# Second expert product as seven products for eight in parts 2 and 3 of a fused attention and MoE kernel, with the forms of the weights kept in DRAM

## The chip, the cores and the metric

One core of a Trainium2 chip runs the whole kernel in one launch. The time is that of the device from start to end, in microseconds (us); the median of several runs counts. PE is the matrix engine (TensorE), DVE the vector engine, ACT the scalar engine, POOL is GpSimd, SP is the engine that issues all transfers of this kernel. SBUF is the memory beside the engines, PSUM the eight banks of 128x512 fp32 into which PE writes, DRAM the device's main memory.

## The reference

An attention over 4 sequences of 768 tokens with 8 heads of 64, in which a query sees the 4 first keys and the 128 last ones, is followed by a mixture of 8 experts over the N = 3072 tokens of dimension D = 512, with hidden size F = 1024. Every token goes through every expert, weighted by a gate that 8 Sinkhorn iterations balance:

```python
x = attention(q, k, v, n_sink=4, window=128)       # [3072, 512]
P = exp(x @ w_gate - max)
for _ in range(8):
    P /= P.sum(1, keepdims=True) + 1e-09
    P /= P.sum(0, keepdims=True) + 1e-09
    P *= N / E
for e in range(E):
    h = maximum(x @ w1[e], 0.0)
    out += P[:, e:e + 1] * (h @ w2[e])
```

The gate weights are never negative, so weighting `h` by them before the second product gives the same sum as weighting the product.

## The kernel before

Every fp32 operand of a large product is split into a high part (a rounded copy in PE's faster format, made on ACT: a CAST) and a low part (the rest, a subtraction on DVE); `split` does both. A product is then three matmuls, high x high, high x low and low x high.

The tokens go in three parts of 1024 (`NPART`), each in two halves of 512 (`HT`). The weights of an expert go in four units (`NU`) of 256 hidden columns (`UF`). While the attention runs, expert 0 is computed for part 1 in a plain way, in small steps between the attention's (`plain`; its additions are L605). Then come 28 units of part 1 and 32 each of parts 2 and 3, in a pipeline of two stages: in one step PE runs the first product of unit n and the second product of unit n-1. The list `STEPS` interleaves them; a scheduler (the framework's, which orders each engine's instructions by priority and its own estimate of times) places the rest.

- `load_unit` loads a unit's two weight blocks (`r1`, `r2`, 512 KB each), makes sums of blocks on POOL (L715 to L718, tile `ST`), and splits everything into `W1f` (seven forms) and `W2f`.
- The first product is Winograd's form of Strassen's algorithm: a unit's two hidden chunks by two halves of D, times two halves of D by two halves of tokens, in seven products M1 to M7 for eight. Each is 6 matmuls of 128x512 (L771), so 42 in a unit. The forms of x^T that they read (`B11`, `B21`, `B22`, `T1` to `T4`) are made once a part (`load_x`, `make_form`, `fill_form`).
- ACT copies M2, M3 and M5 out of PSUM; DVE adds (L784, tile `C`); ACT and DVE make the split relu (`h`, L779 and L780).
- The second product is plain: eight token tiles by two hidden chunks in sixteen steps of 3 matmuls (L832), 48 in a unit. `weigh` adds each tile to `acc` in SBUF, with the gate weight of its tokens as the factor (L844, DVE). After the last unit of a part `acc` goes out.

Each engine runs its own instructions in order, so an instruction that waits holds those behind it. The order also has every transfer wait for the transfer eight before it.

Of the kernel before, what the change touches and what calls it, by code (L numbers as in the profile page):

```python
# [79 lines left out]
def tile_any_span(ctx: ExitStack, tc: tile.TileContext, q, k, v, span, wg, w1, w2, out):  # L80
    """The whole computation for any n_sink and window."""
# [16 lines left out]
    with ExitStack() as ph:  # L98
# [122 lines left out]
def tile_sink_attention_moe(ctx: ExitStack, tc: tile.TileContext, q, k, v, wg, w1, w2, out):  # L221
    """The computation for n_sink = SINK and window = P."""
# [34 lines left out]
    ident = const.tile([P, P], F32, name="ident")  # L257
    make_identity(nc, ident)
    masks = []
    for t in range(3):  # L260
# [448 lines left out]
    def load_unit(e, u):  # L709
# [216 lines left out]
```

## Time and profile before

| | |
|---|---|
| median of 3 runs | 2238.93 us (2238.04 to 2239.73) |
| span of the profiled execution | 2235.5 us (the page has no other time of it) |
| PE busy | 2213.5 us, 99% |
| DVE, ACT, POOL busy | 1588.4, 899.4, 468.7 us |
| DMA | 140.5 MB in 172567 packets, mean 63 GB/s |

The span runs from the first to the last instruction on the core. The profile's matmul lines give a busy time in which pipelined matmuls overlap; what one costs in a full row is read from the chain of waits, which has them end to end. Windows give, for a stretch, its length and each engine's busy time, with the clock, the DMA engines' busy share and the rate.

### The profile page before, as it was taken

What the parts mean: (1) busy time and instruction counts of PE and PEld (TensorE: products, weight loads), DVE (VectorE), ACT (ScalarE), POOL (GpSimd) and SP (SyncE); (2) the same over time, 40 slices, a digit from 0 to 9 for tenths busy, and PEclk for the clock granted to TensorE, in tenths of its full rate; (3) what the DMA queues carried; (4) which work ended last, traced back from release to release, by engine and by line L of the source; (5) the groups of instructions that cost most, each with busy time, mean ns of one, the idle gap of its engine ahead of it and who ended that gap; (6) DMA issues with size and microseconds to landing.
All of it is one profiled execution on the core that took longest, in us unless ns stands there. A gap on an engine that the chain in (4) does not pass through costs nothing.

```text
span 2235.5 us, 29446 instructions
## 1 busy us (share of the span) xinstructions
PE 2213.5 (99%) x10843; PEld 1838.1 (82%) x10843; DVE 1588.4 (71%) x3010; ACT 899.4 (40%) x1970; POOL 468.7 (21%) x851
## 2 busy tenths in 40 slices
PE   7999999999999999999999999999999999999998
PEld 5888887888888888888888888888888888888887
DVE  8877879766766676867666666667766667666765
ACT  7777763333333333433333333334333333333331
POOL 7655642111111111211111111112111111111100
PEclk9999999999999999999999999999999999999999
DMA  6333422111111111311111111111311111111101
GB/s 172 87 81 90 115 84 87 49 56 57 55 40 57 57 50 45 132 57 48 48 57 57 48 47 57 57 44 42 104 57 39 56 57 57 38 57 57 52 25 39
DMA packets 172567, 140.50 MB, mean 63 GB/s; under 512 B 80256, under 2 KB 141696, under 8 KB 172416
## 3 DMA queue, kind: packets, MB, share of 16 engines
q1 hardware_dynamic: 172416, 138.55, 20.6%
q8 instruction: 87, 1.43, 0.3%
q14 instruction: 64, 0.52, 0.1%
HBM read 125.95 MB, written 12.58 MB: 62 GB/s over the span
## 4 chain that ended last, share of the span: by engine, by line
PE 96%; DVE 2%; ACT 1%; DMA 0%; issue 0%; SPq 0%; POOL 0%; DVEq 0%; POOLq 0%; ACTq 0%
PE o L832 45%; PE c L771 39%; PE O L507 3%; PE ps L450 2%; PE g L581 2%; PE pt L471 1%; PE o L597 1%; PE pt L411 1%; PE O L597 1%; ACT sc L456 0%; PE ps L581 0%; DVE sc L453 0%; DVE PT L338 0%; PE O L537 0%; PE pt L487 0%
## 5 line engine op out<-in xcount | busy, mean ns | idle before, releaser
L832 PE MATMUL o<-W2f,h 128*128 128x512 f32 x4416 | 1073.9, 389 | 0.0
L832 PEld LDWEIGHTS o<-W2f,h 128*128 128x128 f32 x4416 | 828.7, 188 | 172.2 <-DVE acc L844 0.2
L844 DVE SCALAR_TENSOR_TENSOR acc<-o,Pt,acc 128x512 f32<-128x512 f32 x720 | 539.0, 750 | 341.4 <-PE o L832 339.5
L771 PE MATMUL c<-T,W1f 128*128 128x512 f32 x2208 | 561.0, 389 | 0.0
L771 PEld LDWEIGHTS c<-T,W1f 128*128 128x128 f32 x2208 | 414.0, 188 | 86.8 <-DVE C L784 1.0
L779 ACT ACTIVATE h<-C 128x512 fp32r<-128x512 f32 x276 | 174.4, 632 | 638.3 <-DVE C L784 627.3
L771 PE MATMUL c<-B,W1f 128*128 128x512 f32 x1656 | 406.7, 389 | 0.0
L715 POOL TENSOR_TENSOR ST<-r 128x256 f32<-128x256 f32 x92 | 70.0, 761 | 1552.1 <-DMA r<-in_moe_w_dram 1052.8
L771 PEld LDWEIGHTS c<-B,W1f 128*128 128x128 f32 x1656 | 310.5, 188 | 64.8 <-ACT M L797 0.4
L784 DVE TENSOR_TENSOR C<-c,M 128x512 f32<-128x512 f32 x276 | 190.7, 691 | 114.6 <-PE c L771 111.5
L780 DVE SCALAR_TENSOR_TENSOR h<-C,h 128x512 fp32r<-128x512 f32 x276 | 190.0, 688 | 2.7 <-ACT h L779 2.7
L801 ACT COPY M<-c 128x512 f32<-128x512 f32 x92 | 54.0, 587 | 307.0 <-PE c L771 307.0
L779 ACT ACTIVATE h<-c 128x512 fp32r<-128x512 f32 x92 | 55.0, 598 | 247.9 <-PE c L771 247.7
L780 DVE SCALAR_TENSOR_TENSOR h<-c,h 128x512 fp32r<-128x512 f32 x92 | 63.6, 691 | 106.6 <-ACT h L779 106.5
L338 DVE TENSOR_TENSOR W1f<-ST,W1f 128x512 fp32r<-128x512 f32 x184 | 119.6, 689 | 0.0
L338 DVE TENSOR_TENSOR W2f<-r,W2f 128x512 fp32r<-128x512 f32 x184 | 119.1, 686 | 0.0
L456 ACT ACTIVATE sc<-sc,st 128x264 f32<-128x264 f32 x192 | 98.2, 512 | 50.4 <-DVE st L453 49.5
L337 ACT CAST W2f<-r 128x512 fp32r<-128x512 f32 x184 | 113.6, 620 | 6.9 <-PE O L597 6.0
L460 POOL TENSOR_SCALAR sc<-sc,st 128x264 f32<-128x264 f32 x192 | 93.9, 500 | 75.5 <-DVE st L458 58.6
L337 ACT CAST W1f<-ST 128x512 fp32r<-128x512 f32 x184 | 105.2, 620 | 0.0
L338 DVE TENSOR_TENSOR W1f<-r,W1f 128x512 fp32r<-128x512 f32 (+1 forms) x184 | 101.0, 549 | 0.0
L507 PE MATMUL O<-PT,V 128*128 128x256 f32 x528 | 85.1, 294 | 0.9 <-DVE xr L519 0.9
(131 smaller groups left out, 1761.7 us busy)
## 6 DMA issues: line engine op xcount, KB each, us to landing
r<-in_moe_w_dram SPq DMA_DIRECT2D x192, 512.0 KB
xscr<-xr SPq DMA_DIRECT2D x24, 256.0 KB
x<-xscr SPq DMA_DIRECT2D x12, 512.0 KB
out_dram<-acc SPq DMA_DIRECT2D x24, 256.0 KB
kr<-in_k_dram SPq DMA_DIRECT2D x23, 256.0 KB
qr<-in_q_dram SPq DMA_DIRECT2D x23, 256.0 KB
vr<-in_v_dram SPq DMA_DIRECT2D x23, 256.0 KB
vs<-in_v_dram SPq DMA_DIRECT2D x24, 4.0 KB
```

Of the source, the lines that this page charges most:

```text
L337: nc.scalar.copy(dst[:, 0], src)
L338: nc.vector.tensor_sub(dst[:, 1], src, f32(dst[:, 0]))
L456: nc.scalar.activation(sc[:, h, :], sc[:, h, :], AF.Exp, bias=nmx[:, h:h + 1], scale=-1.0, accum_out=sm[:, h:h + 1])
L460: nc.gpsimd.tensor_scalar(sc[:, h, :], sc[:, h, :], rs[:, h:h + 1], 1.0, op0=ALU.mult, op1=ALU.mult)
L507: nc.tensor.matmul(u["O"][:, pr], lhsT=x_, rhs=y_, start=(j == 0), stop=(j == len(ops) - 1))
L715: nc.gpsimd.tensor_add(S[:, 0], A21, A22)
L771: nc.tensor.matmul(ps, lhsT=W1[:, a, i, k, :], rhs=XF[fb][:, b, k, :], start=(start and j == 0), stop=(stop and j == len(ops) - 1), skip_g ...
L779: nc.scalar.activation(h[key][:, 0], src, AF.Relu)
L780: nc.vector.scalar_tensor_tensor(h[key][:, 1], src, 0.0, f32(h[key][:, 0]), op0=ALU.max, op1=ALU.subtract)
L784: nc.vector.tensor_add(C, c1, m)
L832: nc.tensor.matmul(o, lhsT=h[c, th][:, a, off:off + P], rhs=W2[:, w, c, :], start=(c == 0 and j == 0), stop=(c == 1 and j == 2))
L844: nc.vector.scalar_tensor_tensor(acc[i], o_, Pt[:, i, e:e + 1], acc[i], op0=ALU.mult, op1=ALU.add)
```

## The change

Attention, the plain expert and the arithmetic of part 1 stay. What changes:

**Memory.** The tiles of attention are in pools that are closed before part 1, and the pools of part 1 lie over that space. They wait tile by tile for what lay there.

**Part 1** still loads, sums and splits weights, and its second product is still plain. In addition each unit's 14 forms, high and low, are written to DRAM: `W1f` (seven forms for the first product) and, for the second product, three blocks of `W2f` and four sums T1 to T4, made on POOL and split into a tile `WT` with one buffer. Expert 0's four units, which part 1 doesn't compute, are loaded, made and written beside the units n = 5, 11, 17, 23. Beside n = 2, 8, 14, 20 `keep_forms` makes a quarter each of part 3's x^T forms and writes them (`xfs`). The gate weights are transposed on PE and written (`psd`).

**Parts 2 and 3** load the forms ready-made, in tiles of 256 KB: seven `W1q` and seven `W2q` a unit. The gate weight, spread over the partitions (`PB`), is multiplied into the relu (L993, L1038), then the second product takes seven products for eight too: two hidden chunks by two halves of tokens, times two chunks by two halves of D. The sums S1 to S4 of the hidden blocks are made on POOL (L1023, L1029, L1032, L1040), and each of the seven forms is split into `hf` (ACT L341, DVE L342). A group of two units makes 14 steps of 6 matmuls (L1071), in output that is transposed (D on the partitions). The steps' results are summed over the whole part, four of the 14 in their PSUM banks (`HELD`), ten in SBUF (L1079, DVE). At a part's end DVE combines them (`together`), and PE transposes them back in 64 pieces of 128x128 (`put_out`, L1113), for ACT to copy and SP to store.

The core of the diff:

```diff
+    early.close()
+    xtp = ctx.enter_context(tc.tile_pool(name="xtp", bufs=1, reuse_waits="tile"))
...
+        w1p, w2p, hp = pool_("w1p", 2), pool_("w2p", 2), pool_("hp0", 2)
+        cp, rawp, sp, wtp, xrp = pool_("cp", 1), pool_("rawp0", 2), pool_("sp", 1), pool_("wtp", 1), pool_("xrp", 1)
...
         def load_unit(e, u):
...
+            T = sp.tile([P, 4, HD], F32, name="TT")
+            nc.gpsimd.tensor_sub(T[:, 0], B12, B11)
+            nc.gpsimd.tensor_sub(T[:, 1], B22, T[:, 0])
+            nc.gpsimd.tensor_sub(T[:, 2], B22, B12)
+            nc.gpsimd.tensor_sub(T[:, 3], B21, T[:, 1])
+            WT = wtp.tile([P, 2, 4, HD], F32R, name="WT")
+            for c in range(2):
+                split(WT[:, :, 2 * c:2 * c + 2], T[:, 2 * c:2 * c + 2])
...
+            for w in range(2):
+                nc.sync.dma_start(d1[:, :, w], f32(W1[:, w]).rearrange("p a k f -> p a (k f)"))
+                nc.sync.dma_start(d2[:, 0, w], f32(W2[:, w, 0, 0:HD]))
+                nc.sync.dma_start(d2[:, 1:3, w], f32(W2[:, w, 1]).rearrange("p (a d) -> p a d", d=HD))
+                nc.sync.dma_start(d2[:, 3:7, w], f32(WT[:, w]))
...
+        for n, step in enumerate(steps + [None]):
...
+                W = load_unit(*step)
+                if n % 6 == 5 and n // 6 < NU:
+                    load_unit(0, n // 6)
+                if n % 6 == 2 and n // 6 < 4:
+                    keep_forms(2, n // 6)
...
+            def summed(key, m, th):
+                w = T[key] = wp.tile([P, HT], F32, name="w")
+                nc.vector.tensor_add(w, T["c1"], T[m])
+                nc.vector.scalar_tensor_tensor(w, w, 0.0, PB[:, th], op0=ALU.max, op1=ALU.mult)
...
+            def p7():
+                run("M7", T["c1"], False)
+                summed("A22", "M5", 1)
+                nc.gpsimd.tensor_add(T["A21"], T["A21"], T["A22"])
+                form("S1", T["A21"])
+                form("A22", T["A22"])
+                nc.gpsimd.tensor_sub(T["A11"], T["A21"], T["A11"])
+                form("S2", T["A11"])
...
+            for m, k in order:
+                held = (m, k) in HELD
+                if not held or begin:
+                    o = bank()
...
+                for j, (a, w, (e, u, F)) in enumerate((a, w, g) for g in group for a, w in ((0, 0), (0, 1), (1, 0))):
+                    nc.tensor.matmul(o, lhsT=W2[m, u][:, a, k * P:(k + 1) * P], rhs=F[H_OF[m]][:, w, :],
...
+                if not held:
+                    if begin:
+                        t = sums[m, k] = (accq if (m, k) in FEW else accp).tile([P, DM], F32, name="acc")
+                        nc.scalar.copy(t, o)
+                    else:
+                        nc.vector.tensor_add(sums[m, k], o, sums[m, k])
...
+        STEPS2 = ["M2", "M1", "M5", "second", "M3", "second", "M6", "second", "second", "M7", "second", "second", "M4", "second"]
```

How it moves instructions, at three places. A row names the line, the operation and output<-inputs.

The start of part 1 on DVE, where the plain expert's last addition (`acc<-O,acc`) meets part 1's first splits and the Sinkhorn steps (`rsum`, `csum`, `Pt`). Before:

```order
L338 TENSOR_TENSOR T_5613<-x_5582,T_5613 128x2x256
L43 RECIPROCAL rsum<-rsum 128x24
L338 TENSOR_TENSOR T_5613<-x_5582,T_5613 128x2x256
L44 TENSOR_TENSOR Pt<-Pt,rsum 128x192
L338 TENSOR_TENSOR W1f<-r_5618,W1f 128x512
L46 TENSOR_REDUCE csum<-Pt 128x8
L587 SCALAR_TENSOR_TENSOR h_5392<-ps,h_5392 128x256
L605 TENSOR_TENSOR acc<-O,acc 128x512
L338 TENSOR_TENSOR W1f<-r_5618,W1f 128x256
L338 TENSOR_TENSOR W1f<-ST,W1f 128x512 x2
```

The addition shown and three more of the plain expert, the last 25 rows further, follow splits of T and `W1f`. After:

```order
L611 TENSOR_TENSOR acc<-O,acc 128x512
L44 TENSOR_TENSOR Pt<-Pt,rsum 128x192
L342 TENSOR_TENSOR T_5606<-x_5598,T_5606 128x2x256
L46 TENSOR_REDUCE csum<-Pt 128x8
L342 TENSOR_TENSOR T_5606<-x_5598,T_5606 128x2x256
L51 TENSOR_SCALAR csum_5694<-o 128x8
L342 TENSOR_TENSOR T_5615<-x_5602,T_5615 128x2x256
L52 RECIPROCAL csum_5694<-csum_5694 128x8
L342 TENSOR_TENSOR T_5615<-x_5602,T_5615 128x2x256
L53 SCALAR_TENSOR_TENSOR Pt<-Pt,csum_5694 128x192
L342 TENSOR_TENSOR T_5622<-x_5600,T_5622 128x2x256
```

The last addition now comes first, then eight splits of T forms (two each of four) among Sinkhorn steps, then, seven rows on, the first of `W1f`.

Part 1 in its run, on ACT, over a unit's step; names in brackets are the semaphores waited for, DMAHW0 to DMAHW7 those of transfers. Before (a step of another unit, with no wait for a transfer but those of the loads):

```order
L789 COPY M_8311<-c_8310 128x512 [waits PE_49,Activation_49]
L337 CAST W2f<-r_8443 128x512
L779 ACTIVATE h_8314<-C 128x512 [waits DVE_49]
L797 COPY M_8313<-c_8309 128x512 [waits PE_49,Activation_49]
L801 COPY M_8312<-c_8309 128x512 [waits PE_49,Activation_49]
L779 ACTIVATE h_8315<-C 128x512 [waits DVE_49]
L779 ACTIVATE h_8316<-C 128x512 [waits DVE_49]
L779 ACTIVATE h_8317<-c_8308 128x512 [waits PE_49]
L337 CAST W1f<-r_8597 128x512 [waits DMAHW4_49]
L337 CAST W1f<-r_8597 128x256
L337 CAST W1f<-ST 128x512 [waits Pool_49] x2
L337 CAST W2f<-r_8599 128x512 [waits DMAHW5_49,PE_49]
```

After, beside `keep_forms` (`r_8320` holds its x blocks):

```order
L341 CAST WT<-r_8320 128x256 [waits DMAHW2_49,DMAHW5_49,DMAHW1_49,DMAHW7_49,DMAHW0_49,DVE_49]
L849 COPY M_8358<-c_8357 128x512 [waits PE_49]
L341 CAST W1f<-ST 128x512 [waits Pool_49]
L839 ACTIVATE h_8361<-C 128x512 [waits DVE_49]
L857 COPY M_8360<-c_8356 128x512 [waits PE_49]
L341 CAST WT<-r_8320 128x512 [waits DMAHW0_49,DMAHW7_49,Activation_49,Pool_49]
L861 COPY M_8359<-c_8356 128x512 [waits PE_49]
L839 ACTIVATE h_8362<-C 128x512 [waits DVE_49]
L341 CAST WT<-r_8320 128x512 [waits DMAHW5_49,DMAHW4_49,DMAHW6_49,DMAHW3_49,Activation_49]
L839 ACTIVATE h_8363<-C 128x512 [waits DVE_49]
L341 CAST WT<-TT 128x512 [waits DMAHW1_49,DMAHW2_49,DMAHW0_49,DMAHW3_49,Activation_49,Pool_49]
L341 CAST WT<-TT 128x512 [waits Pool_49]
```

Four casts into the single `WT` (three from x blocks, then the unit's own, `WT<-TT`) now stand here between the copies `M` and the relus `h` and wait for transfers; the first of the x blocks' four stands a few rows ahead. On DVE, where the `W1f` that follows an extra unit is split, the same appears:

```order
L844 TENSOR_TENSOR C<-c_7792,M_7795 128x512 [waits PE_49,Activation_49]
L840 SCALAR_TENSOR_TENSOR h_7798<-C,h_7798 128x512 [waits Activation_49]
L894 SCALAR_TENSOR_TENSOR acc<-o,Pt,acc 128x512 [waits PE_49] x3
L844 TENSOR_TENSOR C<-c_7792,M_7796 128x512 [waits PE_49,Activation_49]
L342 TENSOR_TENSOR W1f<-r_7925,W1f 128x512 [waits DMAHW3_49,DMAHW2_49,Activation_49]
L894 SCALAR_TENSOR_TENSOR acc<-o,Pt,acc 128x512 [waits PE_49]
L840 SCALAR_TENSOR_TENSOR h_7799<-C,h_7799 128x512 [waits Activation_49]
```

The row `W1f<-r_7925` waits for the stores of the extra unit's `W1f`, with the next additions of `acc` and `h` behind it.

The steady units, on DVE. Before, a unit:

```order
L338 TENSOR_TENSOR W2f<-r_11942,W2f 128x512 x2
L780 SCALAR_TENSOR_TENSOR h_11813<-C,h_11813 128x512
L844 SCALAR_TENSOR_TENSOR acc<-o,Pt,acc 128x512 x3
L784 TENSOR_TENSOR C<-c_11807,M_11811 128x512
L844 SCALAR_TENSOR_TENSOR acc<-o,Pt,acc 128x512
L780 SCALAR_TENSOR_TENSOR h_11814<-C,h_11814 128x512
L844 SCALAR_TENSOR_TENSOR acc<-o,Pt,acc 128x512
L784 TENSOR_TENSOR C<-c_11807,M_11812 128x512
L844 SCALAR_TENSOR_TENSOR acc<-o,Pt,acc 128x512
L780 SCALAR_TENSOR_TENSOR h_11815<-C,h_11815 128x512
L844 SCALAR_TENSOR_TENSOR acc<-o,Pt,acc 128x512
L780 SCALAR_TENSOR_TENSOR h_11816<-c_11807,h_11816 128x512
```

After, the first unit of a pair in part 2 or 3:

```order
L342 TENSOR_TENSOR hf<-w,hf 128x512
L1079 TENSOR_TENSOR acc<-b,acc 128x512
L992 TENSOR_TENSOR w<-b,M_15741 128x512
L993 SCALAR_TENSOR_TENSOR w<-w,PB 128x512
L1079 TENSOR_TENSOR acc<-b,acc 128x512
L342 TENSOR_TENSOR hf<-w,hf 128x512
L1079 TENSOR_TENSOR acc<-b,acc 128x512
L992 TENSOR_TENSOR w<-b,M_15699 128x512
L993 SCALAR_TENSOR_TENSOR w<-w,PB 128x512
L342 TENSOR_TENSOR hf<-w,hf 128x512 x3
L1079 TENSOR_TENSOR acc<-b,acc 128x512
L1038 SCALAR_TENSOR_TENSOR w<-b,PB 128x512
```

The splits of weights are gone, splits of `hf` are in, and after three of them, the last of which needs POOL's S1 and S2, an addition `acc<-b,acc` stands that frees a PSUM bank. PE in the same stretch has, after:

```order
L721 MATMUL b<-T_10943,W1q 128x512 x6
L1071 MATMUL b<-hf,W2q 128x512 x6
L721 MATMUL b<-B_10806,W1q 128x512 x6
L721 MATMUL b<-B_10834,W1q 128x512 x6
L721 MATMUL b<-T_10859,W1q 128x512 x6
L1071 MATMUL b<-hf,W2q 128x512 x6
L721 MATMUL b<-B_10892,W1q 128x512 x6
L1071 MATMUL b<-hf,W2q 128x512 x6
L721 MATMUL b<-T_10923,W1q 128x512 x6
L1071 MATMUL b<-hf,W2q 128x512 x12
L721 MATMUL b<-T_10938,W1q 128x512 x6
L1071 MATMUL b<-hf,W2q 128x512 x12
```

Between two first products there now stand one or two steps of six matmuls, where before two to four steps of three stood.

More of the change, by code (lines that the diff above doesn't have):

```diff
@@ L258, in tile_sink_attention_moe @@
     make_identity(nc, ident)
+    ones = const.tile([P, P], F32, name="ones")
+    nc.vector.memset(ones, 1.0)
+    early = ctx.enter_context(ExitStack())
+    attc = early.enter_context(tc.tile_pool(name="attc", bufs=1))
     masks = []
     for t in range(3):
-        m = const.tile([P, CW], F32, name=f"mask{t}")
+        m = attc.tile([P, CW], F32, name=f"mask{t}")
         nc.gpsimd.memset(m, 0.0)
@@ L326, in tile_sink_attention_moe, with load_raw @@
     NU = FF // UF
-    def load_raw(e, u):
+    def load_raw(rawp, e, u):
         r1 = rawp.tile([P, KC, UF], F32, name="r1")
@@ L818, in tile_sink_attention_moe @@
-    READS = {"M1": "B11", "M2": "B21", "M3": "B22", "M4": "T4", "M5": "T1", "M6": "T2", "M7": "T3"}
-    STEPS = ["M2", "M1", "M5"] + ["second"] * 4 + ["M3"] + ["second"] * 2 + ["M6"] + ["second"] * 4 + ["M7"] + ["second"] * 4 + ["M4"]
-    def second(W, h, job):
-        _, W2 = W
-        part, e, u = job
-        for t in list(range(TH // 2, TH)) + list(range(TH // 2)):
-            th, off = divmod(t * P, HT)
-            o = pso.tile([P, DM], F32, name="o")
-            for c in range(2):
-                for j, (a, w) in enumerate(((0, 0), (0, 1), (1, 0))):
-                    nc.tensor.matmul(o, lhsT=h[c, th][:, a, off:off + P], rhs=W2[:, w, c, :],
-                                     start=(c == 0 and j == 0), stop=(c == 1 and j == 2))
-                if c == 1:
-                    weigh(e, part * TH + t, o, part > 0 and e == 0 and u == 0, e == E - 1 and u == NU - 1)
-                yield
@@ L838, in weigh @@
-    def weigh(e, i, o_, fresh, done):
-        assert weighted
-        if fresh:
-            acc[i] = accp.tile([P, DM], F32, name="acc")
-            nc.vector.tensor_scalar(acc[i], o_, Pt[:, i, e:e + 1], None, op0=ALU.mult)
-        else:
-            nc.vector.scalar_tensor_tensor(acc[i], o_, Pt[:, i, e:e + 1], acc[i], op0=ALU.mult, op1=ALU.add)
-        if done:
-            nc.sync.dma_start(out[i * P:(i + 1) * P, :], acc[i])
-    def sinkhorn_step():
-        with tc.high_priority():
-            if next(sk, 0) == 0 and not weighted:
-                weighted.append(True)
-                for t in range(TH):
-                    nc.vector.tensor_scalar(acc[t], acc[t], Pt[:, t, 0:1], None, op0=ALU.mult)
@@ L856, in tile_sink_attention_moe @@
-    weighted = []
-    sk_psum = lambda shape: pso.tile(shape, F32, name="o")
-    load_x(0)
-    make_form("T1")
-    fill_form("T1")
-    make_form("T2")
-    for form in ("T2", "T3", "T4"):
-        fill_form(form)
-    steps = [(part, e, u) for part in range(3) for e in range(E) if (part, e) != (0, 0) for u in range(NU)]
-    pending = []
-    refill = False
-    prev = None
-    for step in steps + [None]:
-        first_steps, second_steps = None, iter(())
-        if step is not None:
-            part, e, u = step
-            refill = (e, u) == (E - 1, NU - 1) and part < 2
-            W = load_unit(e, u)
-            if refill:
-                load_x(part + 1)
-            first_steps, h = stages(W)
-        if prev is not None:
-            second_steps = second(*prev)
-        for s_ in STEPS:
-            if s_ == "second":
-                next(second_steps, None)
-            elif first_steps:
-                first_steps[s_]()
-            if s_ != "second":
-                sinkhorn_step()
-                if refill:
-                    pending.append(READS[s_])
-                if len(pending) > 2 or pending and not refill:
-                    fill_form(pending.pop(0))
-        for _ in second_steps:
@@ L893, in tile_sink_attention_moe @@
             pass
-        prev = None if step is None else (W, h, step)
 _INS = ["q", "k", "v", "n_sink", "window", "moe_w_gate", "moe_w1", "moe_w2"]
```

431 lines of the change are left out of this document (333 added, 98 removed).

## The prediction

> **What bounds the kernel now.** I read the page's busy shares first, then its chain, then the same chain in order of time, then the groups by form.
>
> ```profile
> span 2235.5 us, 29446 instructions
> PE 2213.5 (99%) x10843; PEld 1838.1 (82%) x10843; DVE 1588.4 (71%) x3010; ACT 899.4 (40%) x1970; POOL 468.7 (21%) x851
> PEclk9999999999999999999999999999999999999999
> q1 hardware_dynamic: 172416, 138.55, 20.6%
> HBM read 125.95 MB, written 12.58 MB: 62 GB/s over the span
> PE 96%; DVE 2%; ACT 1%; DMA 0%; issue 0%; SPq 0%; POOL 0%; DVEq 0%; POOLq 0%; ACTq 0%
> 423.72 4.08 PE c L771 x18
> 444.12 4.08 PE c L771 x18
> 2217.55 12.25 PE o L832 x54
> ```
>
> TensorE is the bound, at an undiminished clock: 99% busy and 96% of the chain. In the chain, three leading first products (18 matmuls of 128x512) take 4.08 us, so one matmul costs 4.08 / 18 = 0.2267 us; the 54 second-product matmuls give 12.25 / 54 = 0.2269. (The groups' mean of 389 ns is pipelined time and isn't used.) The next unit's block starts 20.40 us later, and 90 matmuls (42 + 48) x 0.2267 are 20.40: a unit has no gap. So a matmul removed from a steady stage is worth its full 0.2267 us as long as the other engines and the DMA queue keep pace. A stretch of such units, the crowded stretch at the start of part 1 and the densest transfer bursts read:
>
> ```profile
> 1110.00:1500.00 390.00, 390.00 (x1723) 322.92 (x1722) 264.36 (x402) 133.82 (x247) 54.56 (x76) 1.00 0.16 52
> 349.69:382.80 33.11, 32.22 (x142) 24.64 (x141) 30.85 (x77) 16.31 (x31) 6.33 (x9) 1.00 0.27 80
> 611.00:612.00 1.00, 1.00 (x6) 0.83 (x5) 1.00 (x3) 1.00 (x2) 0.00 (x0) 1.00 0.96 332
> 614.00:615.00 1.00, 1.00 (x6) 0.84 (x5) 0.75 (x1) 0.00 (x0) 0.92 (x3) 1.00 0.91 350
> 921.00:923.00 2.00, 2.00 (x11) 1.65 (x10) 1.64 (x4) 0.59 (x1) 0.00 (x0) 1.00 1.03 380
> ```
>
> The columns are the span, busy PE, PEld, DVE, ACT and POOL, clock, DMA share, GB/s. The DMA engines are 16% busy in the steady units and saturate at 332 to 380 GB/s; DVE is at 68% there, but at 93% (30.85 of 33.11) at the start of part 1.
>
> **The change, term by term.** Durations that the terms use, by form:
>
> ```profile
> L338 DVE TENSOR_TENSOR W1f<-ST,W1f 128x512 fp32r<-128x512 f32 x184 | 119.6, 689 | 0.0
> L337 ACT CAST W1f<-ST 128x512 fp32r<-128x512 f32 x184 | 105.2, 620 | 0.0
> L338 DVE TENSOR_TENSOR T<-x,T 128x512 fp32r<-128x512 f32 x24 | 15.7, 684 | 0.0
> L716 POOL TENSOR_TENSOR ST<-ST,r 128x256 f32<-128x256 f32 x92 | 72.5, 788 | 0.0
> L717 POOL TENSOR_TENSOR ST<-r 128x256 f32<-128x256 f32 x92 | 70.0, 761 | 0.0
> L485 POOL TENSOR_TENSOR SS<-sc,SS 128x16 fp32r<-128x16 f32 x48 | 11.8, 245 | 0.0
> L471 PE MATMUL pt<-ident,sc 128*128 128x128 f32 x352 | 56.0, 278 | 4.7 <-DVE Q L338 1.3 <-DVE PT L338 1.2 <-POOL sc L460 1.0
> ```
>
> *Second product, -87.0.* In the 64 units of parts 2 and 3 it falls from 48 matmuls to 42: 384 x 0.2267 = 87.0 us, all on the chain.
>
> *Turning the output back, +10.4.* The sums now stand transposed: 64 transposes of 128x128 at the ends of the parts, each 56.0 / 352 = 0.159 us, are 10.2, and two for the gate weights make 10.4. Nothing on PE can hide PE work.
>
> *Work taken away from the other engines, 0.* In parts 2 and 3 the weight splits go (on DVE four W1f and two W2f subtractions in a unit, all but one 512 wide, about 3.9 us) and seven form splits come. By the order DVE runs 19 operations in a unit there; at 0.69 us they are 13.1 us of the new unit's 84 x 0.2267 = 19.04. Covered while PE sets the pace; if it weren't, DVE could lose 5.9 us a unit before it became the bound.
>
> *Start of part 1, +10 (4 to 18).* In the order the splits of T1 to T4 and of the first W1f stood ahead of the last addition of the plain expert, and now stand behind it, because their space is that of attention. The trace of before shows where that point is, and what PE did there:
>
> ```profile
> 348.64 2.45 PE L771 MATMUL c<-B,W1f 128*128 128x512 f32 x10
> 349.14 0.63 DVE L605 TENSOR_TENSOR acc<-O,acc 128x512 f32<-128x512 f32 x1
> 382.80 3.62 DVE L854 TENSOR_SCALAR acc<-acc,Pt 128x512 f32<-128x512 f32 x8
> ```
>
> PE went straight on at 348.64. Now the eight T subtractions (8 x 0.684 = 5.5), the first W1f one (0.69) and the Sinkhorn steps standing between them (some 3.3, by the same steps' rows ahead of 349.69) come after 349.77, so the first low part of W1f is there near 359. About 12 matmuls that read high parts only (2.7 us) can run meanwhile: 10 - 2.7 = 7. The same surplus on a DVE that is 93% busy pushes the end of Sinkhorn, and so the weighting at 382.80, back by about 6, partly the same delay: together 10; 4 if the 7% slack and the ACT side absorb half, 18 if they add up.
>
> *Storing the forms in part 1, +12 (0 to 60).* This is the largest unknown.
>
> ```profile
> r<-in_moe_w_dram SPq DMA_DIRECT2D x192, 512.0 KB
> ```
>
> A unit still loads two such blocks, 1.05 MB, and now stores 14 forms of 256 KB: 4.72 MB. With four extra units of expert 0 and four quarters of part 3's x forms (2.4 MB each) part 1 moves about 163 MB, 285 GB/s over its 28 x 20.4 = 571 us. The rows of before saturate at 332 to 380, so the mean fits, at 75 to 86% of them, if rows of 1 KB written go like rows read (of before's traffic, 12.58 of 138.5 MB are written). What doesn't fit is local: at n = 5, 11, 17, 23 two units' traffic (9.4 MB, 25 to 28 us) falls into one. W1f's next buffer then waits for the extra unit's stores, and WT has a single buffer, so the casts on ACT and the subtractions on DVE stand in their queues until stores land; behind them stand the copies of M3 and the C additions that PE's next product waits for. Placing the stores by hand, the wait is 0 to 2 us at most of the eight events; I take 1.5 x 8 = 12. The lower end is full cover; the upper is 7.5 us an event, the excess of 28 over 20.4 unhidden each time.
>
> *Part 1 to 2, +5 (1 to 12).* Two units of first products run with no second product beside them: 7 x 1.36 = 9.5 us of PE, 14 DVE operations, 9.7 us, and 28 loads of 256 KB, 7.3 MB, in 19 us, 385 GB/s. All three limits meet; a tenth of each unit and some arrival time lost is 5, 1 if only DVE counts, 12 if loads go at 250.
>
> *Part 2 to 3, +2 (0 to 6).* Seven 1 MB loads of x forms (7.3 MB, 19 to 22 us) each follow the last reading of their block, a unit ahead of use; the transposes and the output fill the time.
>
> *Pairs in parts 2 and 3, +9 (0 to 30).* By hand from the order: in the first unit of a pair M7 ends after ten blocks, at 13.60 of 19.04. Then 0.1 to DVE, two DVE steps (1.4), S1 and S2 on POOL, the cast of S2 (0.62), its subtraction (0.69), and only then, in DVE's queue, the addition (0.69) that frees the bank that M1 of the second unit needs at 20.40. POOL's 512-wide step isn't in the trace: 245 + (761 - 245) x 496/240 = 1.31 us, 1.52 if two 256-wide ones. That gives 19.7, or 20.1, and with five handoffs about 20.1: just in time. But POOL and DVE can slow each other:
>
> ```profile
> 344.70 1.22 DVE L338 TENSOR_TENSOR W1f<-ST,W1f 128x512 fp32r<-128x512 f32 x1
> 345.34 1.19 POOL L716 TENSOR_TENSOR ST<-ST,r 128x256 f32<-128x256 f32 x1
> ```
>
> Beside each other they took 1.22 and 1.19 where their means are 0.69 and 0.79. Two stretched POOL steps and one DVE step add 0.4 + 0.4 + 0.5 = 1.3, 1.0 past the slack: 30 pairs x 1.0 = 30. I take 0.3 a pair, 9, since most steps in the quiet rows keep their mean.
>
> *Tail, +3 (1 to 5).* After the last product come an addition, four copies and four stores where one addition and one store stood; the last transposes are counted above.
>
> Sum: -87.0 + 10.4 + 10 + 12 + 5 + 2 + 9 + 3 = -35.6. Against the profiled span 2235.5 that is 2199.9. The page gives the span alone; the median of the runs, 2238.93, stands 3.4 above it, so I forecast 2203.
>
> **Rivals.**
>
> *Everything that isn't PE work is hidden.* With stores and pairs at 0 the sum is -56.6: 2182; with every term at its lower end 2168. For it: 16% DMA share and 68% DVE now. Against it: part 1 needs five times the present traffic.
>
> *POOL and DVE take turns.* If every S1 and S2 collides, the pairs cost 30 instead of 9: 2224. The two rows speak for it; against it, the means of L716 (788) and L717 (761) show that collisions are rare where POOL runs beside a DVE at 68%. [...]
>
> *Slower: stores bound part 1.* Without the store term the sum is -47.6, so the kernel is slower once part 1 takes 47.6 us more than 571: once 163 MB go at less than 163 / 619 = 263 GB/s. At 240 part 1 takes 679, +108, and the time is 2299; just past the point, 2245. For it: no row of before shows mostly written traffic, single buffers stop the queues for turnarounds, and every transfer waits for the one eight before it. Against it: 380 GB/s where reads and output stores mixed.
>
> *The change doesn't do what it says:* the removed matmuls were not on the chain, or sums held in banks over a part stall PE as much as is saved. Then the time is within 5 us of before. Against it stands the gapless 20.40 us unit.
>
> **How the numbers follow.** Forecast (2190 to 2218) 0.58; all hidden (2168 to 2190) 0.16; taking turns (2218 to 2234) 0.12; stores bound part 1 (above 2243) 0.10; no effect 0.04. Faster by over 0.2% (4.5 us, about what a measurement here can tell from no change) is 0.58 + 0.16 + 0.12 + 0.01 = 0.87, within it 0.03, slower 0.10. The range 2170 to 2236 leaves out the slower rival, most of the no-effect case and the last of the hidden one.
>
> **What would show it.** In the changed profile: six-matmul blocks following each other by 1.36 us and a unit of 19.04 in parts 2 and 3, against 19.3 to 20 with waits of PE on DVE's addition if pairs cost more; a PE gap of 7 to 10 us after the plain expert's last addition; units of 20.4 in part 1, longer ones after n = 2 and n = 5, with casts of WT and W1f released by stores; DMA shares near 0.8 in part 1 and 0.5 after. I am wrong if part 1's ordinary units exceed 21.5 us, if POOL's 512-wide step takes over 1.8 us, or if PE in the steady pairs waits for W1q or W2q.

## The result, and the profile after

The changed kernel takes 2258.47 us (median of 4 runs, 2256.15 to 2259.48) against 2239.21 before (4 runs): 1.0086 of the time before, 95% interval 1.0072 to 1.0101. It is slower by 19.3 us, where I had forecast 2203. The profiled run, 2257.83, has a span of 2255.9. The page's first lines and the queue's:

```profile
span 2255.9 us, 31869 instructions
PE 2169.5 (96%) x10525; PEld 1781.6 (79%) x10525; DVE 1654.8 (73%) x2973; ACT 892.8 (40%) x1908; POOL 780.8 (35%) x1011
q1 hardware_dynamic: 394240, 451.20, 64.6%
HBM read 313.64 MB, written 137.46 MB: 200 GB/s over the span
```

The page lists 318 PE instructions fewer (384 fewer second-product matmuls, 66 transposes more), but PE is busy only 44 us less, where the sum had 76.6, and it stands idle for 86 us instead of 22. In the other 32 us of the 76.6 the matmuls that are left are shown as taking longer; up to about half of that is the clock, as the last section shows, and the rest isn't broken down.

Where the time went is read from the starts of the units: the first of every 42 first-product matmuls, in both traces. Unit 4 of part 1 starts at 423.56 before and at 441.64 after; its last unit, 27, at 892.75 and at 953.71. The windows over these 23 units, which are 469.2 us at 20.40, before (first line) and after, and over 29 units of part 2, after (552.2 at 19.04):

```profile
423.56:892.75 469.19, 469.19 (x2071) 388.51 (x2070) 317.85 (x484) 161.86 (x300) 65.92 (x92) 1.00 0.16 52
441.64:953.71 512.07, 483.76 (x2071) 392.71 (x2070) 402.50 (x574) 209.33 (x388) 211.89 (x224) 0.98 0.80 262
1028.94:1592.98 564.04, 556.61 (x2438) 456.43 (x2436) 384.73 (x545) 173.38 (x297) 149.74 (x116) 1.00 0.65 201
```

The second line is 42.9 us too long, the third 11.9. The whole account, against the terms of the prediction:

| | forecast | measured |
|---|---|---|
| second product, transposes | -76.6 | -76.6 (the counts are as expected) |
| up to unit 4 of part 1 | +10 | +18.1 (1.9 of it in attention's first 40 us) |
| storing the forms, units 4 to 27 of part 1 | +12 | +42.9 |
| part 1 to 2 | +5 | +5.9 |
| pairs in parts 2 and 3 | +9 | +22.9 |
| part 2 to 3 | +2 | +6.4 |
| tail | +3 | +1.1 |
| sum | -35.6 | +20.7 (span: +20.4) |

Each measured entry is the time between two such starts less what its matmuls take at 0.2267 us (and its transposes at 0.159). How part 1 loses time is seen at unit 10, while the extra unit of n = 11 is made (572 to 597 us). The timeline of all engines, cut to the chain:

```profile
579.47 1.25 SPq L336 DMA_DIRECT2D r<-in_moe_w_dram  x1
587.28 0.74 POOL L752 TENSOR_TENSOR TT<-r 128x256 f32<-128x256 f32 x1 [11.14 <-DMA r<-in_moe_w_dram]
588.68 0.73 POOL L753 TENSOR_TENSOR TT<-r,TT 128x256 f32<-128x256 f32 x1
589.45 0.62 ACT L341 CAST WT<-TT 128x512 fp32r<-128x512 f32 x1 [4.78 <-POOL TT L753]
590.10 1.82 DVE L342 TENSOR_TENSOR WT<-TT,WT 128x512 fp32r<-128x512 f32 x2 [3.38 <-ACT WT L341]
591.84 0.68 DVE L844 TENSOR_TENSOR C<-c,M 128x512 f32<-128x512 f32 x1
592.58 2.22 PE L721 MATMUL c<-T,W1f 128*128 128x512 f32 x6 [2.57 <-DVE C L844]
```

A weight load issued at 579.47 lands near 587; POOL's sums `TT` follow; ACT's cast into `WT` has waited 4.78 us for them and DVE's subtraction 3.38 for the cast; the C addition behind it on DVE is what PE's next product needs; PE waits 2.57 us, and its six matmuls then take 2.22 us instead of 1.52.

The same wait also reaches PE through ACT. At unit 13, in the timeline from 636 to 668, cut to the chain:

```profile
647.90 0.62 ACT L341 CAST WT<-TT 128x512 fp32r<-128x512 f32 x1 [2.39 <-POOL TT L753]
648.43 0.62 ACT L839 ACTIVATE h<-C 128x512 fp32r<-128x512 f32 x1
648.96 0.57 ACT L857 COPY M<-c 128x512 f32<-128x512 f32 x1
649.58 1.66 PE L721 MATMUL c<-B,W1f 128*128 128x512 f32 x6 [3.08 <-ACT M L857]
```

The copy `M` stands in ACT's order behind the cast that waits for POOL. Over the 23 units PE waits 15.1 us for this copy (12 times) and 13.2 us for the C addition (8 times), and ACT's casts into `WT` wait 54.9 us for POOL's sums (20 times).

The pairs, in the timeline from 1284 to 1306, first PE's rows (the first unit of this pair starts at 1281.53):

```profile
1300.57 1.52 PE L721 MATMUL b<-B,W1q 128*128 128x512 f32 x6
1302.62 1.67 PE L721 MATMUL b<-B,W1q 128*128 128x512 f32 x6 [0.53 <-DVE acc L1079]
```

and, of the same timeline, the engines that PE waits for:

```profile
1295.40 0.69 DVE L1079 TENSOR_TENSOR acc<-b,acc 128x512 f32<-128x512 f32 x1
1296.00 0.68 DVE L992 TENSOR_TENSOR w<-b,M 128x512 f32<-128x512 f32 x1
1297.55 1.28 POOL L1029 TENSOR_TENSOR w<-w 128x512 f32<-128x512 f32 x1 [3.45 <-DVE w L993]
1298.91 1.29 POOL L1032 TENSOR_TENSOR w<-w 128x512 f32<-128x512 f32 x1
1299.52 2.44 DVE L342 TENSOR_TENSOR hf<-w,hf 128x512 fp32r<-128x512 f32 x3 [2.11 <-ACT hf L341]
1301.89 0.68 DVE L1079 TENSOR_TENSOR acc<-b,acc 128x512 f32<-128x512 f32 x1
```

M2 of the second unit starts in time at 1300.57, M1 at 1302.62 instead of 1301.93, after the addition that follows the three hf splits. Units alternate between 19.04 and 19.87 to 19.91 us. By form, what the two engines take in these parts:

```profile
L342 DVE TENSOR_TENSOR hf<-w,hf 128x512 fp32r<-128x512 f32 x448 | 369.0, 846 | 265.2 <-ACT hf L341 249.3
L1029 POOL TENSOR_TENSOR w<-w 128x512 f32<-128x512 f32 x64 | 82.6, 1291 | 217.0 <-DVE w L993 214.9 <-DMA W1q<-w1s 2.1
```

POOL's 512-wide step takes 1.29 us, as estimated; the hf subtractions take 0.85 instead of 0.69.

### The profile page after: what moved, and what is told of

It reads as the page before. It is cut to its first block, busy times and chain, and to the rows that moved or that the text cites. A ratio compares the mean times of both kernels' runs of the same rounds, so it can differ in the third digit from the quotient of the medians.

```text
span 2255.9 us, 31869 instructions
## 1 busy us (share of the span) xinstructions
PE 2169.5 (96%) x10525; PEld 1781.6 (79%) x10525; DVE 1654.8 (73%) x2973; ACT 892.8 (40%) x1908; POOL 780.8 (35%) x1011
## 5 line engine op out<-in xcount | busy, mean ns | idle before, releaser
L1071 PE MATMUL b<-hf,W2q 128*128 128x512 f32 x2688 | 661.1, 390 | 0.0
L1071 PEld LDWEIGHTS b<-hf,W2q 128*128 128x128 f32 x2688 | 505.4, 188 | 104.7
L341 ACT CAST hf<-w 128x512 fp32r<-128x512 f32 x448 | 271.7, 621 | 798.5 <-POOL w L1023 297.1
L342 DVE TENSOR_TENSOR hf<-w,hf 128x512 fp32r<-128x512 f32 x448 | 369.0, 846 | 265.2 <-ACT hf L341 249.3
L721 PE MATMUL b<-T,W1q 128*128 128x512 f32 x1536 | 390.8, 390 | 0.7 <-DVE w L992 0.7
L721 PEld LDWEIGHTS b<-T,W1q 128*128 128x128 f32 x1536 | 288.2, 188 | 62.1 <-DVE w L992 2.0
L890 PE MATMUL o<-W2f,h 128*128 128x512 f32 x1344 | 330.8, 394 | 0.8 <-DVE acc L894 0.8
L721 PE MATMUL b<-B,W1q 128*128 128x512 f32 x1152 | 292.8, 394 | 20.0 <-DVE acc L1079 14.9
L890 PEld LDWEIGHTS o<-W2f,h 128*128 128x128 f32 x1344 | 256.1, 191 | 55.2 <-DVE acc L894 1.2
L1023 POOL TENSOR_TENSOR w<-w 128x512 f32<-128x512 f32 x64 | 82.7, 1292 | 565.7 <-DVE w L993 553.4
L721 PEld LDWEIGHTS b<-B,W1q 128*128 128x128 f32 x1152 | 214.0, 188 | 76.6 <-DVE acc L1079 26.7
L1079 DVE TENSOR_TENSOR acc<-b,acc 128x512 f32<-128x512 f32 x300 | 204.9, 683 | 28.6 <-PE b L1071 28.6
L721 PE MATMUL c<-T,W1f 128*128 128x512 f32 x672 | 176.7, 398 | 16.4 <-DVE C L844 16.4
L894 DVE SCALAR_TENSOR_TENSOR acc<-o,Pt,acc 128x512 f32<-128x512 f32 x224 | 164.5, 744 | 36.7 <-PE o L890 36.3
L1029 POOL TENSOR_TENSOR w<-w 128x512 f32<-128x512 f32 x64 | 82.6, 1291 | 217.0 <-DVE w L993 214.9
L721 PE MATMUL c<-B,W1f 128*128 128x512 f32 x504 | 131.0, 405 | 17.4 <-ACT M L857 15.1
L1040 POOL TENSOR_TENSOR w<-w 128x512 f32<-128x512 f32 x64 | 83.4, 1302 | 176.5 <-DVE w L1038 172.8
L993 DVE SCALAR_TENSOR_TENSOR w<-w,PB 128x512 f32<-128x512 f32 x192 | 135.1, 703 | 6.3
```

The source lines that it names most:

```text
L341: nc.scalar.copy(dst[:, 0], src)
L342: nc.vector.tensor_sub(dst[:, 1], src, f32(dst[:, 0]))
L721: nc.tensor.matmul(ps, lhsT=w1(a, k), rhs=x[:, b, k, :], start=(start and j == 0), stop=(stop and j == len(TERMS) - 1), skip_group_check=n ...
L890: nc.tensor.matmul(o, lhsT=h[c, th][:, a, off:off + P], rhs=W2[:, w, c, :], start=(c == 0 and j == 0), stop=(c == 1 and j == 2))
L894: nc.vector.scalar_tensor_tensor(acc[t], o, Pt[:, t, e:e + 1], acc[t], op0=ALU.mult, op1=ALU.add)
L993: nc.vector.scalar_tensor_tensor(w, w, 0.0, PB[:, th], op0=ALU.max, op1=ALU.mult)
```

## The experiments

Each is the changed kernel with one edit unless told otherwise, and all ratios are to the kernel before, on the same chip. Differences in us are to the 2258.47 above. Runs of one kernel spread over up to 7 us, so a difference of less than 3 us is read neither as a gain nor as a loss.

**e1: no stores.** Is it the traffic?

```diff
+            if (e, u) != (1, 0):
+                w1s[e, u], w2s[e, u] = w1s[1, 0], w2s[1, 0]
+                return W1, W2
             d1 = w1s[e, u] = dram.tile(...)
```

> Only the first unit's forms are stored in part 1; parts 2 and 3 load that one unit's forms each time, so their traffic is unchanged and only part 1's stores (117 of 137 MB written) go; all sums and splits stay. Theory A, that part 1's units lengthen because the weight loads come late behind the stores in the transfer queue, so that casts and subtractions that need them hold up ACT and DVE: the 43 us by which 24 units of part 1 exceed 20.4 us go almost wholly, 2215 to 2222. Rival B, that the added splits, sums and extra units themselves are too much for ACT, DVE and POOL in order: at most 10 us go, 2248 or more.

2255.65 us, 1.0079 (1.0062 to 1.0096): 2.8 us less than with all stores, where theory A asked for 36 or more. It fell. The window over the same 23 units:

```profile
443.81:951.83 508.02, 483.85 (x2072) 395.75 (x2071) 380.81 (x571) 207.57 (x385) 181.64 (x216) 0.97 0.22 67
```

and one event of its timeline:

```profile
499.37 0.72 POOL L754 TENSOR_TENSOR TT<-r 128x256 f32<-128x256 f32 x1
500.81 0.62 ACT L341 CAST WT<-TT 128x512 fp32r<-128x512 f32 x1 [4.75 <-POOL TT L753]
501.46 0.69 DVE L342 TENSOR_TENSOR WT<-TT,WT 128x512 fp32r<-128x512 f32 x1 [4.17 <-ACT WT L341]
502.07 0.68 DVE L847 TENSOR_TENSOR C<-c,M 128x512 f32<-128x512 f32 x1
502.81 2.93 PE L721 MATMUL c<-T,W1f 128*128 128x512 f32 x6 [4.27 <-DVE C L847]
```

The DMA engines are 22% busy instead of 80%, and the units still take 508 us for 469. The same chain stands there, POOL, ACT, DVE, PE, with no store near it: POOL does its eight sums one after the other and those for `WT` come last.

**e2: no extra units.**

```diff
                 if n % 6 == 5 and n // 6 < NU:
-                    load_unit(0, n // 6)
+                    w1s[0, n // 6], w2s[0, n // 6] = w1s[1, n // 6], w2s[1, n // 6]
```

> Part 1 does not make expert 0's four units (parts 2 and 3 load expert 1's forms in their place, the same traffic there). Theory A: the excess of the units beside n = 5, 11, 17, 23 and of the second one after each (about 5 and 2 us) goes, 22 us, 2236, and the units beside n = 8, 14, 20 keep their 3.4 to 5 us. Rival, that part 1 is short of mean transfer rate: the whole excess falls, those beside keep_forms too, 2225 or less.

2237.45 us, 0.9997 (0.9988 to 1.0007), 21 us less. The 23 units take 494.9 us, 17 less, and the start gives some 4 more. The size is the one that A had forecast, but it doesn't speak for A: leaving the four units out takes their sums and splits as well as their traffic. The units beside `keep_forms` (7 and 8, 13 and 14, 19 and 20) keep none of their excess, against theory A: they take 20.40 us each, so the order moved with the edit.

**e6: no W2 sums, no WT.** Four sums on POOL and two splits a unit are left out, and parts of W2f are stored in their place.

```diff
-            nc.gpsimd.tensor_sub(T[:, 0], B12, B11)
             ...
-            for c in range(2):
-                split(WT[:, :, 2 * c:2 * c + 2], T[:, 2 * c:2 * c + 2])
...
-                nc.sync.dma_start(d2[:, 3:7, w], f32(WT[:, w]))
+                nc.sync.dma_start(d2[:, 3:7, w], f32(W2[:, w]).rearrange("p c (a d) -> p (c a) d", d=HD))
```

> Neither the four W2 sums nor their splits are made in part 1; the same number of bytes is stored from W2f in their place. Theory B1: the excess beside the extra units goes as with the splits on POOL or more, 2225 to 2232; the units beside keep_forms (n = 8, 14, 20), which splits into the same tile, keep about 3 us. Rival B2: 2250 or more.

2221.05 us, 0.9927 (0.9910 to 0.9943): 37 us less, with every byte still stored. The 23 units:

```profile
440.37:914.91 474.54, 471.12 (x2072) 388.08 (x2070) 350.93 (x520) 179.37 (x334) 105.05 (x116) 1.00 0.86 281
```

474.5 for 469.2, at a DMA share of 0.86 and 281 GB/s, more than the changed kernel's 262. So the stores are hidden, and the sums and splits for `WT` in the engines' orders are the cause. ACT's casts still wait for stores now and then (10.7 us for those of `keep_forms`, 9.4 for those of `W1f`, over the 23 units), and PE loses 5.3 us in all. The units beside `keep_forms` are nearly free too (at most 1.5 us over), which B1 had not said; the time is below its range.

**e9: the W2 sums on DVE.** The work stays, but the splits no longer wait for POOL.

```diff
-            nc.gpsimd.tensor_sub(T[:, 0], B12, B11)
+            nc.vector.tensor_sub(T[:, 0], B12, B11)
 (and the same for the other three)
```

> The four sums of W2's blocks in part 1 are made on DVE instead of POOL (1.7 us a unit more there); their splits stay on ACT and DVE. Theory B1: the splits then stand in DVE's own order behind sums that wait for nothing but the weights that W2f's splits wait for too, so the waits for POOL go, and 43 us of excess in part 1 fall to 15 or less: 2230. Rival B3, that DVE is simply too full in part 1 with WT's work: no gain or a loss, 2255 or more.

2230.50 us, 0.9963 (0.9949 to 0.9977): 28 us less, the time that B1 gave, but only in part by its way. The 23 units:

```profile
436.64:929.29 492.65, 479.15 (x2071) 392.05 (x2070) 429.09 (x682) 208.35 (x388) 109.10 (x116) 0.99 0.83 273
```

They take 492.7 us, 19 less, so 23.5 us of the excess stay where B1 allowed 15; the rest of the gain comes from the start (unit 4 starts at 436.64, 5 earlier) and single stalls after it. DVE is fuller than before (429 of 492.7 us, 87%), so it wasn't too full: it had stood waiting. PE no longer waits for the C addition at all, and 13.4 us for ACT's copy `M` (7 times; 15.1 in the changed kernel). Of the 23.5 us, 13.8 lie at units 8, 14 and 20, beside `keep_forms`, and 8.9 at units 6, 12, 18 and 24; no experiment takes these apart.

**e5: the splits on POOL instead.**

```diff
-                split(WT[:, :, 2 * c:2 * c + 2], T[:, 2 * c:2 * c + 2])
+                nc.gpsimd.tensor_scalar(WT[:, 0, ...], T[...], 1.0, 1.0, op0=ALU.mult, op1=ALU.mult)
+                nc.gpsimd.tensor_sub(WT[:, 1, ...], T[...], f32(WT[:, 0, ...]))
```

> The splits of the W2 sums into WT in part 1 are made on POOL instead of ACT and DVE; stores, sums and extra units stay. Theory B1, that part 1's 43 us of excess come from the WT splits that stand in ACT's and DVE's queues ahead of the copies and C additions while they wait for POOL's sums (and these for late weight loads): the units beside n = 5, 11, 17, 23 fall to 22 or less, 25 us go, 2233. Rival B2, that the amount of work (or loads that arrive late for W1f) is the limit: under 8 us, 2250 or more; slower than 2258 if POOL's longer work slows DVE.

2282.66 us, 1.0205 (1.0188 to 1.0222), 24 us worse. POOL's subtraction alone takes 1.42 us, and POOL is busy for 312 of the 534 us that the 23 units take, instead of 212 of 512. The loss sits in the units after the extra ones (5, 11, 17, 23), which take 31 to 33 us. At unit 5, in the timeline from 455 to 500:

```profile
465.46 3.76 SPq L766 DMA_DIRECT2D w2s<-WT  x2
472.00 1.27 SPq L763 DMA_DIRECT2D w1s<-W1f  x2
480.42 0.92 ACT L341 CAST W1f<-r 128x512 fp32r<-128x512 f32 x2 [10.77 <-DMA w1s<-W1f]
485.39 0.68 DVE L845 TENSOR_TENSOR C<-c,M 128x512 f32<-128x512 f32 x1
486.12 2.93 PE L721 MATMUL c<-T,W1f 128*128 128x512 f32 x6 [7.63 <-DVE C L845]
```

SP issued in order here too. The store of `WT` waits for POOL's splits (over the 23 units 159 us for L758, 27 times), and the store of the extra unit's `W1f` stands behind it. So that buffer comes free late, ACT's cast into it waits (52.2 us in 4 times, against 10.9 in the changed kernel), and the C addition that PE needs is late. My version of B1 was too simple: the splits left ACT's and DVE's orders, but the stores behind them in SP's order still waited for POOL. This is the wait for stores that the prediction had charged; here the stores are issued late because of what stands ahead of them.

**e3: one bank more for the pairs.**

```diff
-        HELD = (("M1", 0), ("M5", 0), ("M6", 0), ("M3", 0))
+        HELD = (("M1", 0), ("M5", 0), ("M6", 0))
```

> Three of the fourteen sums stay in PSUM banks over a part instead of four, so five banks go round instead of four, for one more addition on DVE a pair. Theory C, that the 0.85 us by which each second unit of a pair starts M1 late is the wait for the bank that DVE's addition behind three hf splits frees: pairs take 38.1 us, 24 us go, 2234. Rival D, that DVE and POOL slow each other and the chain of the hidden forms is late for itself: pairs stay at 38.9, 2257 to 2262.

2259.50 us, 1.0093 (1.0076 to 1.0110): nothing gained, so C in this form fell. The wait changed its name and is smaller but comes in every unit (19.44 us each, pairs of 38.9 as before):

```profile
1304.71 1.65 PE L721 MATMUL b<-B,W1q 128*128 128x512 f32 x6 [0.46 <-ACT M L987]
```

M3 now waits for ACT's copy of M5, and ACT's copies stand behind casts of hf that wait for POOL. The bank was only where the lateness showed.

**e4: the hidden forms on DVE.**

```diff
-                nc.gpsimd.tensor_add(T["A21"], T["A21"], T["A22"])
+                nc.vector.tensor_add(T["A21"], T["A21"], T["A22"])
 (and the same for the other three)
```

> S1 to S4 of the hidden blocks are made on DVE instead of POOL (23 operations a unit there, 15.9 us of 19.04 at 0.69). If the collisions of the two engines lengthen hf (0.85 us against 0.69), hf falls to 0.69 and the pair's wait of 0.85 us goes: 2234. If DVE becomes too full, units of 19.5 or more and 2265 or later.

2226.16 us, 0.9939 (0.9922 to 0.9955): 32 us less, faster than before by itself. The window over part 2's 29 units:

```profile
1026.68:1578.86 552.18, 552.18 (x2438) 457.36 (x2436) 427.23 (x663) 168.79 (x296) 0.00 (x0) 1.00 0.67 205
```

and hf among its groups by form:

```profile
L342 DVE TENSOR_TENSOR hf<-w,hf 128x512 fp32r<-128x512 f32 x448 | 297.6, 688 | 69.4 <-ACT hf L341 68.9
```

29 units in 552.18 us, 19.04 each, with PE busy throughout; hf is back at 0.69. DVE carries some 79 us more of forms in these units (29 times four steps of 0.68) and is only 42.5 us busier (427.23 for 384.73), since its other steps no longer lose time to POOL. The 9 us beyond the 22.9 of the pairs are at the ends of the parts (unit 27 to 31: 71.5 us instead of 75.2; unit 60 to 63: 62.7 instead of 68.6).

**e10: e9 and e4 together.**

> The same with the hidden forms of parts 2 and 3 on DVE as well. The two causes are separate: 2226 - 28 = 2198. If B3 holds, 2225.

2198.19 us, 0.9822 (0.9805 to 0.9838): 40 us faster than before and 60 faster than the change as it was made. The gains add, 28 + 32. Parts 2 and 3 run at 19.04 us a unit; the 23 units of part 1 still take 488.9 us for 469.2, and unit 4 starts at 434.50, 10.9 later than before.

**The start of part 1: e7, e11, e13, e14.** e7 allocates part 1's pools in another order, so that the first weights lie over attention's space; e11 makes the low parts of the first T forms on POOL; e13 has ACT copy something into their place; e14 runs four Sinkhorn iterations.

```diff
e7   hp, w2p, cp, wtp = ...; sp, w1p, rawp, xrp = ...   (the order of allocation alone)
e11  + nc.gpsimd.tensor_sub(t[:, 1, :, c], src[:, :, c], f32(t[:, 0, :, c]))
e13  + nc.scalar.copy(t[:, 1, :, c], src[:, :, c])
e14  - for _ in range(8):
     + for _ in range(4):
```

> The pools of part 1 are only allocated in another order: the tiles that the first units need at once (W1f, the raw weights, the x blocks) lie over attention's space, freed earlier, instead of over the plain expert's. If the first splits of W1f behind the plain expert's last addition are what costs at the start, PE's first products begin within 2 us of the plain expert's end, and the start of part 1 loses 8 us less: 2250. If the T splits alone (still behind it) set it, no change.

> Only the low parts of the first T1 to T4 of part 1 are made on POOL, which is idle there, instead of DVE. If DVE's queue behind the plain expert's last addition sets the start, the first low part of W1f comes 4 to 5 us earlier and the start loses 6 to 8 us less: 2251. If the loads of the first units (which wait for the plain expert's space) set it, no change: 2258.

> The first T1 to T4 of part 1 get a second copy from ACT in the place of their low parts, which leaves the subtractions out (part 1's arithmetic changes by that) and frees 5.5 us of DVE's queue at the start without giving POOL work. If DVE's queue is what holds PE up at the start, unit 4 of part 1 starts 6 to 9 us earlier (441.6 in the changed kernel, 423.6 before) and the time is 2250; if not, 2257 to 2260.

> Four Sinkhorn iterations instead of eight (this leaves out part of the computation), which takes some 11 us of small DVE steps and the serial chain of DVE and PE out of the start of part 1. If the chain's end, and with it the weighting that the second products wait for, sets the start, unit 4 starts 12 us earlier or more: 2246 or less. If only the splits behind the plain expert's last addition count, 4 us or less: 2254.

| | us | ratio, interval | unit 4 starts at |
|---|---|---|---|
| changed kernel | 2258.47 | 1.0086 (1.0072 to 1.0101) | 441.64 |
| e7 | 2264.79 | 1.0117 (1.0100 to 1.0134) | 442.57 |
| e11 | 2260.01 | 1.0101 (1.0084 to 1.0118) | 442.07 |
| e13 | 2261.03 | 1.0099 (1.0082 to 1.0115) | 443.83 |
| e14 | 2252.49 | 1.0064 (1.0047 to 1.0081) | 436.55 |

Taking the T subtractions off DVE doesn't shorten the start, so my account of it, DVE's queue behind the last addition, isn't the cause by itself. In the changed kernel DVE's last addition, PE's two longest waits and the first low part of W1f read:

```profile
353.62 0.63 DVE L611 TENSOR_TENSOR acc<-O,acc 128x512 f32<-128x512 f32 x1
355.58 0.39 PE L49 MATMUL o<-csum,ones 128*128 128x8 f32 x2 [2.15 <-DVE csum L46]
360.82 0.69 DVE L342 TENSOR_TENSOR W1f<-r,W1f 128x512 fp32r<-128x512 f32 x1
361.57 1.22 PE L721 MATMUL c<-B,W1f 128*128 128x512 f32 x2 [2.29 <-DVE W1f L342]
```

DVE works from 352.0 to 367.6 with no pause of over 0.2 us, so e11's rival, late loads, isn't what holds it there. In e13 PE's waits read:

```profile
353.68 0.39 PE L49 MATMUL o<-csum,ones 128*128 128x8 f32 x2 [1.67 <-DVE csum L46]
356.83 0.58 PE L49 MATMUL o<-csum,ones 128*128 128x8 f32 x2 [2.76 <-DVE csum L46]
360.15 0.60 PE L49 MATMUL o<-csum,ones 128*128 128x8 f32 x2 [2.75 <-DVE csum L46]
360.61 0.78 PE L721 MATMUL c<-B,W1f 128*128 128x512 f32 x1
```

With less on DVE the scheduler put three small Sinkhorn products ahead of part 1's first product on PE, and each waits for a round of DVE steps. In e7 the first products start straight after the plain expert (353.67), and PE then stands before such a product for 3.77 us. Halving the iterations gives 5 us at unit 4, less than half of the 12 that the chain theory asked for and just over the 4 of the other. So the start is a chain of DVE and PE that run in order, in which each experiment moved the wait. What the 16 us consist of beyond that stays open.

**e8 and e12: combinations.** e8 is e4, e5 and e7; e12 is e10 and e11.

> Hidden forms on DVE, WT splits on POOL and the other order of the pools together. If the three causes are separate, 2226 - 25 - 8 = 2193; if POOL's work was only hidden by idle time that DVE now uses, 2210 or more.

> The three moves together: 2198 - 7 = 2191, or 2198 if the start doesn't move.

e8 takes 2263.68 us, 1.0116 (1.0099 to 1.0133), undone by e5's edit; the three changes one by one would add up to 2257, and the 7 us beyond that aren't explained. e12 takes 2201.14, 0.9839 (0.9822 to 0.9855), no better than e10, as e11 alone gained nothing.

## Why the prediction was wrong, step by step

- *Second product, transposes, bound by PE:* right. e4's and e10's parts 2 and 3 run at 19.04 us a unit with PE always busy.
- *Storing the forms in part 1, +12 (0 to 60):* this is the step that failed most, by 31 us, and its mechanism too. I charged the stores' traffic and the waits for stores in `W1f` and the single `WT`. e1 took the traffic away and gained 2.8 us at most; e6 kept it, took the sums and splits for `WT` away, and gained 37. The price lies in an instruction chain that crosses POOL, ACT and DVE once a unit and stands in ACT's and DVE's orders ahead of what PE needs. I had the place right, the casts and subtractions of `WT` ahead of the copies and the C additions, but not what they wait for: POOL's sums have no term in the forecast; they were put at nothing, without a reason. There is room for the work on each engine (DVE is 79% busy in those units), but the chain's end came late. That the wait for POOL is what costs is shown for about half, the 19 us that e9 takes out of these units. For the rest e6 shows only that it goes with `WT`'s sums and splits. The mean rate was right: 0.80 of the DMA engines and 262 GB/s, where the prediction had "near 0.8".
- *The slower rival*, stores that bound part 1, ended on the right side for the wrong reason: e6 stores everything at 281 GB/s and is faster than before.
- *Pairs, +9 (0 to 30):* right mechanism, undersized; 22.9. The chain ended 21.0 us into the first unit instead of 20.1: the A22 addition starts 0.8 us late behind another addition on DVE (1295.40 in the rows above), and the three hf splits take 2.44 us. Of the 1.0 us a pair that collisions of POOL and DVE would cost I had taken 0.3, "since most steps in the quiet rows keep their mean"; those rows are of a POOL that works 2.9 of 20.4 us on short steps, and here it works 5.2 of 19.4 on long ones. The stretch fell otherwise than I had put it: POOL's steps kept their 1.29 us, and DVE's splits alone got longer. The rival in which POOL and DVE take turns was the better forecast for this term: hf at 0.85 against 0.69 once POOL's steps are gone. The seven hf splits of a unit are longer by 23% in the mean. L993's three steps stay at 0.69 in the median, and in the timeline from 1284 to 1306 they fall outside POOL's steps; an addition of L1079 that began there at 1292.65 and ran mostly beside POOL's step from 1292.81 to 1294.10 took 0.68 all the same.
- *Start of part 1, +10 (4 to 18):* 18.1, at its upper end. The first low part of W1f came at 360.8, near the 359 worked out, but by luck: the plain expert's last addition ended at 354.25 instead of 349.77, and DVE began the W1f split 6.6 us after it, where the sum had 8.8. e11 and e13 show that taking that work away doesn't bring the time back.
- *Part 1 to 2* (5.9 for 5) and the *tail* (1.1 for 3) came out; *part 2 to 3* (6.4 for 2) slightly past its end; in e4, where POOL makes no hidden forms, 0.4 of it is left.
- *The chances:* I gave 0.10 to slower, all of it to one mechanism. Five of the six uncertain terms were each taken below the middle of their ranges, so there was more room for the sum to come out slower than faster.

## What to carry to other kernels

Work that is to be hidden has to be priced by when its last input comes and what stands behind it in each in-order engine, not by the free share of the engine: a 1.4 us pair of splits that waited 3 to 4 us for sums on POOL, with the sums and casts before it, cost 37 us, and 117 MB of stores less than 3. In e5 the engine that issues transfers acted as such an in-order engine too: a cast waited 10.77 us for a store that stood behind a late one. In this kernel a short chain that stays on one engine was cheaper than the same work spread over idle ones: giving the busiest of the three engines more to do mended the pairs wholly and part 1's units by about half. When an experiment moves a wait from one name to another and the time doesn't fall (e3, e7, e11, e13), look for the common step ahead of both waits.

## What the runs showed of the hardware that was not expected

In the changed kernel the granted clock fell to half (0.50) after some of PE's gaps. Windows at four of these places read:

```profile
361.30:368.13 6.83, 6.56 (x16) 5.22 (x17) 6.16 (x17) 2.21 (x4) 0.00 (x0) 0.50 1.07 375
501.30:504.70 3.40, 3.40 (x10) 2.64 (x9) 2.04 (x3) 0.63 (x2) 0.00 (x0) 0.50 1.01 335
593.50:596.90 3.40, 3.40 (x10) 2.66 (x9) 2.37 (x4) 1.93 (x4) 1.01 (x1) 0.51 0.41 144
1620.90:1624.30 3.40, 3.40 (x10) 2.62 (x9) 2.06 (x4) 1.20 (x2) 0.00 (x0) 0.50 0.17 33
```

Ahead of the kernel's end there are ten such stretches of 3.41 us (two of them joined at 361.3): one at 26.8, which can bring most of the 1.9 us that attention lost, three at the start of part 1, five in its units, one at part 3's; hence the mean clock of 0.992. Where PE has full rows in them, its 128x512 matmuls start every 0.427 us in the trace instead of every 0.227, so a stretch loses 1.6 us; the ten lose up to 16 us to the clock alone, on top of the gaps themselves, and five of them put some 8 us into the 42.9 of part 1's units. The kernel before has none but at its very end (0.50 from 2233.65 on, with PE idle).

The length of the gap alone doesn't decide. By the trace's record of the clock the slow stretches start at 26.84, 361.35, 392.07, 501.29, 593.45, 726.57, 784.60, 863.11 and 1620.86, each a whole number of steps of 3.413 us, the length that the record gives a single stretch, from the others: they lie on one grid, whatever the time of the gaps. In part 1's units, each of the five slow stretches follows a window of this grid in which PE stood idle for 58 to 74% of the time, by gaps of 1.98 to 3.07 us. The two longest gaps there, 3.08 us from 646.50 and 3.30 us from 916.28, lie across a line of the grid, leave no window idle for more than 55%, and were followed by full speed (1.00). At the start of part 1, with its small products, a window that was idle for 46% was followed by a slow one, so no single share of idle time separates the two here. With the 1.6 us of such a stretch on top, a stall that costs 2.5 us by the waits can so cost 4.1.
